# Weight units converted in turn, three weight fetches in front of v's loads, and column sums by bfloat16 matmuls, in a fused attention and feed-forward kernel

## The chip, the core and the metric

The kernel is one program on one core of one Trainium2 chip. The metric is the device time of an execution in microseconds (us). Before the change the median of 3 runs is 866.14 us (863.68 to 867.47). Everything read from a trace below is from one further execution, which took 866.7 us; its first to last instruction spans 865.0 us, so 1.7 us lie around the span.

## What is computed

Random-feature attention over 8 batches, 8 heads, 576 rows of 64 and 128 features, and behind it a bilinear feed-forward block over the 4608 rows of 512:

```python
def phi(x):
    proj = np.einsum('bhsd,md->bhsm', x, omega)
    sq = np.sum(x * x, axis=-1, keepdims=True) / 2.0
    h = proj - sq
    h = h - np.max(h, axis=-1, keepdims=True)
    return np.exp(h) / np.sqrt(m)
q_p, k_p = (phi(q_s), phi(k_s))            # q, k times 64 ** -0.25
kv = np.einsum('bhsm,bhsd->bhmd', k_p, v)
z = np.sum(k_p, axis=2)
num = np.einsum('bhsm,bhmd->bhsd', q_p, kv)
den = np.einsum('bhsm,bhm->bhs', q_p, z)[..., None] + 1e-06
x = num / den                              # heads side by side: 4608 x 512
a = x @ w1                                 # w1, w2: 512 x 1024
b = x @ w2
h = a * b @ w3                             # 1024 x 1024
out = h @ w_out                            # 1024 x 512
```

The four weight matrices arrive as float64, q, k, v and omega as float32.

## The kernel before

**Tiles.** The 4608 rows are 36 chunks of 128. For each chunk the k side makes features (`features`, `k_chunk`), `kv_batch` sums k features times v over a batch of 4.5 chunks, the q side makes features (`q_chunk`), a transposing DMA on the SP queue turns them (`eqT`), `q_attend` multiplies them with `kv` (the tile `nu`), `x_turn` scales and turns the result (`xT`), `gate` makes x @ w1 and x @ w2 (the tiles `ab`, line 636) and their product, and `project_out` multiplies that with the folded matrix w3 @ w_out (the tiles `o`, line 665). Most products run as three float16 passes over a high and a low part; the first 9 chunks of k and the first 5 of q are multiplied in float32 instead (line 276).

**Weights.** A weight unit is 1 MB of float64. `from_float64` fetches it with a DMA issued by ACT (line 486) into one of three raw buffers of the tile `arena`, takes the absolute value on ACT (line 494, two buffers), and puts a float32 together in four VectorE instructions (lines 500, 502, 503, 504). There are 20 units, and the string `ORDER` says in which order they come: `o` is a quarter of w_out, `W` an eighth of w3, `1` and `2` a quarter of w1 and of w2, `a`, `b` and `S` the splits into float16 parts (`w12_split`, `W_split`). A `W` unit has a float32 product with w_out behind it on TensorE (`product`, the tiles `wp`, lines 574 and 576), whose result ACT copies (line 588). A `1` or `2` unit has its magnitudes summed by a matmul with ones (line 528); the split waits for that sum. A unit's five steps are a tick apart (`SKEW`), and `PER` says how many ticks each slot of the attention's plan takes.

**Norms.** `power_of_two` (line 162) turns sums of squares into a power of two by which q, k, v, omega or the folded matrix are scaled. The sum over the 128 partitions is a matmul of a 128 x 128 float32 matrix of ones with 1, 3 or 8 float32 columns (line 165).

**Order.** `put` files each step in a slot of a plan, the loop at line 812 emits weights, gate units and plan in turn, and the program's scheduler then sets each engine's own order, which the engine keeps. A DMA issued by ACT or SP stands in that engine's queue like any other instruction: one that waits holds up all behind it. The tile `om_raw` of omega's parts lies in `Wb`, and its norm and split stand at the program's head (lines 200 to 206). `v_load` puts v's chunks on the SP queue.

Of the kernel before, what the change touches and what calls it, by code (L numbers as in the profile page):

```python
# [9 lines left out]
F32 = mybir.dt.float32  # L10
F16 = mybir.dt.float16
BF16 = mybir.dt.bfloat16
I32 = mybir.dt.int32
U32 = mybir.dt.uint32
AF = mybir.ActivationFunctionType
ALU = mybir.AluOpType
# [3 lines left out]
P = 128  # L20
# [21 lines left out]
DK = "1111111110"  # L42


ORDER = "ooWWWW11a22booWWWW11a22bS"
SKEW = [0, 1, 2, 3, 4]

PER = [3, 1, 0, 1, 0, 1, 1, 0, 1, 0, 1, 1, 0, 1, 1, 0, 1, 1, 1, 1, 1] + 12 * [1]
# [4 lines left out]
EARLY = 6  # L53
KV_LAG = 5
K_LATE = 8
RAW64_BUFS = 3
O_BUFS = 2
RAW_BUFS = 2
# [10 lines left out]
def tile_favor_attention_then_bilinear_ffn(  # L69
# [19 lines left out]
    nc = tc.nc  # L89
# [12 lines left out]
    SCALE = 1.0 / math.sqrt(math.sqrt(D))  # L102
    TOK = GROUP * P

    const = ctx.enter_context(tc.tile_pool(name="const", bufs=1))
# [9 lines left out]
    def bank_m(name):  # L115
        return ps_m.tile([P, 512], F32, tag="pm", name=name)
# [5 lines left out]
    make_identity(nc, ident)  # L122
    ones_bf = const.tile([P, P], BF16, name="ones_bf")
    nc.vector.memset(ones_bf, 1.0)
    ones = const.tile([P, P], F32, name="ones")
    nc.vector.memset(ones, 1.0)
    ln_e = const.tile([P, 1], F32, name="ln_e")
    nc.vector.memset(ln_e, 15 * math.log(2.0))

# [22 lines left out]
    def square_sum(out, src, name, pre=1.0):  # L152

        n = src.shape[1] * (src.shape[2] if len(src.shape) > 2 else 1)
        junk = at.tile([P, 512], BF16, tag="junk", name=f"junk_{name}", bufs=1)
        r0, rows = 0, src.shape[0]
        dst = junk[r0 : r0 + rows, 0:n]
        if len(src.shape) > 2:
            dst = dst.rearrange("p (i j) -> p i j", i=src.shape[1])
        nc.scalar.activation(dst, src, AF.Square, scale=pre, accum_out=out)  # L160

    def power_of_two(cols, n, name, pre=1.0, add=False, bufs=4):

        bank = bank_m(f"norm_{name}")
        nc.tensor.matmul(bank[:, 0:n], ones, cols, start=True, stop=True)
        t = bank[:, 0:n]
        if add:
            total = small("total")
            nc.vector.tensor_reduce(total, t, AX.X, ALU.add)
            t, n = total, 1  # L170

        q = bank[:, 16 : 16 + n]
        p = bank[:, 32 : 32 + n]

        nc.vector.tensor_scalar(
            q.bitcast(I32), t.bitcast(I32), 24, 23, ALU.logical_shift_right, ALU.logical_shift_left
        )
        nc.vector.tensor_scalar(p, q, 2.0**50 / pre, 2.0**-77 / pre, ALU.mult, ALU.max)
        s = small(f"s{n}_{bufs}", n, bufs=bufs)
        nc.vector.reciprocal(s, p)  # L180
        return p, s
# [13 lines left out]
    om_raw = Wb[:, 0, 0:M]  # L195
    nc.sync.dma_start(om_raw[0:D], omT)
    nc.sync.dma_start(om_raw[D:P], omT)
    om = const.tile([P, 2, M], F16, name="om")
    om_sq = const.tile([P, 1], F32, name="om_sq")
    square_sum(om_sq, om_raw, "om")  # L200
    pom, som = power_of_two(om_sq, 1, "om")
    nc.scalar.mul(om[:, 0], om_raw, som)
    nc.vector.scalar_tensor_tensor(om[:, 1], om_raw, som, om[:, 0], ALU.mult, ALU.subtract)

    unom = const.tile([P, 1], F32, name="unom")
    nc.vector.tensor_scalar_mul(unom, pom, SCALE)

    def chunks_of(b):

# [5 lines left out]
    def load(src, c, name):  # L215
        t = at.tile([P, NP, P], F32, tag=f"{name}raw", name=f"{name}raw_{c}", bufs=RAW_BUFS)
        nc.sync.dma_start(t, src[c])
        raws[name, c] = t
# [39 lines left out]
    def features(c, name):  # L258


        if whole(c, name):
            raw, es = raws.pop((name, c)), SCALE
        else:
            hl, es = hls.pop((name, c))
        pg = banks(f"{name}pj_{c}").rearrange("p g (i m) -> p g i m", m=M)
        pj = pg.rearrange("p g i m -> p (g i) m")

        def project(first=None):
            for i in range(NP):
                if first is not None:  # L270
                    for g in range(2):
                        nc.tensor.matmul(pg[:, g, i], ident, first(g * NP + i), start=True, stop=False)
                if whole(c, name):
                    for g in range(2):
                        d = slice(g * D, (g + 1) * D)
                        nc.tensor.matmul(  # L276
                            pg[:, g, i], raw[d, i], om_raw[d], start=first is None, stop=True
                        )
                    continue
                for n, (x, y) in enumerate(PASSES):  # L280
                    for g in range(2):
                        d = slice(g * D, (g + 1) * D)
                        nc.tensor.matmul(  # L283
                            pg[:, g, i],
                            hl[d, x, i],
                            om[d, y],
                            start=first is None and n == 0,
                            stop=n == len(PASSES) - 1,
                        )

        project()
        if whole(c, name) and c + 2 < NCH:
            load(srcs[name], c + 2, name)
        nm = small("nm", H)
        nc.vector.tensor_reduce(nm, pj, AX.X, ALU.max, negate=True)  # L295
        e = at.tile([P, H, M], F32, tag="e", name=f"{name}e_{c}", bufs=2)
        kind = pick(DK if name == "k" else DQ, c)
        if kind == "2":

            project(lambda h: nm[:, h : h + 1].broadcast_to([P, M]))  # L300
            nc.scalar.activation(e, pj, AF.Exp, scale=es, bias=ln_e)
        elif kind == "1":

            nc.vector.tensor_scalar(nm, nm, es, 15 * math.log(2.0), ALU.mult, ALU.add)
            for h in range(H):
                nc.scalar.activation(e[:, h], pj[:, h], AF.Exp, scale=es, bias=nm[:, h : h + 1])
        else:
            nc.vector.tensor_tensor(e, pj, nm.unsqueeze(2).broadcast_to([P, H, M]), ALU.add)  # L308
            nc.scalar.activation(e, e, AF.Exp, scale=es, bias=ln_e)  # L309
        return e  # L310
# [9 lines left out]
    ek, vhl, vraw, pv, kvs = {}, {}, {}, {}, {}  # L320

    def k_chunk(c):
        e = features(c, "k")
        ek[c] = at.tile([P, 2, H, M], F16, tag="ek", name=f"ek_{c}", bufs=EK_BUFS)
        in_parts(ek[c], e, pick(EH, c), pick(EL, c))

    def v_load(c):
        vraw[c] = at.tile([P, H, D], F32, tag="vraw", name=f"vraw_{c}", bufs=VRAW_BUFS)
        nc.sync.dma_start(vraw[c], v[c])

    vam, sv = {}, {}

# [135 lines left out]
        return free.pop(0)  # L468

    left = {}  # L470

    def used(at):

# [4 lines left out]
    def from_float64(new, src, name):  # L478

        st = {}  # L480

        def fetch():
            at = st["at"] = raw_at.pop(0)
            raw = arena[:, at : at + 4].bitcast(U32).rearrange("p b i -> p (b i)")

            nc.scalar.dma_start(raw.rearrange("p (j i) -> p j i", j=src.shape[1]), src)
            st["raw"] = raw.rearrange("p (i t) -> p i t", t=2)

        def magnitude():

            at = st["mag"] = mag_at.pop(0)
            st["g"] = arena[:, at : at + 2].rearrange("p b i -> p (b i)")
            st["dst"] = new()
            nc.scalar.activation(st["g"], st["raw"][:, :, 1].bitcast(F32), AF.Abs)

        def bits():
            g = st["g"]
            top, low = st["raw"][:, :, 1], st["raw"][:, :, 0]

            nc.vector.tensor_scalar(g, g, F64_TOP, F64_LEAST, ALU.min, ALU.max)  # L500
            g = g.bitcast(U32)
            nc.vector.tensor_scalar(g, g, 3, 0x3FFFFFFF, ALU.logical_shift_left, ALU.bitwise_and)
            nc.vector.scalar_tensor_tensor(g, top, 0xC0000000, g, ALU.bitwise_and, ALU.bitwise_or)  # L503
            nc.vector.scalar_tensor_tensor(  # L504
                st["dst"].bitcast(U32), low, 29, g, ALU.logical_shift_right, ALU.bitwise_or
            )
            raw_at.append(st["at"])
            mag_at.append(st["mag"])

        return [fetch, magnitude, bits]  # L510
# [203 lines left out]
    units, seen = [], {}  # L714
    for ch in ORDER:
        n = seen.get(ch, 0)
        seen[ch] = n + 1
        st = make[ch](n)
        units.append([None] * 3 + st + [None] if len(st) == 1 else st + [None] * (5 - len(st)))
    behind = sorted(range(5), key=lambda k: -SKEW[k])  # L720
    ticks = [
        [units[t - SKEW[k]][k] for k in behind if 0 <= t - SKEW[k] < len(units) and units[t - SKEW[k]][k]]
# [17 lines left out]
    def put(slot, rank, fn):  # L740
        plan.setdefault(slot, []).append((rank, len(plan[slot]) if slot in plan else 0, fn))
# [65 lines left out]
        step(i)  # L807
    for c in range(2):
        load(kT, c, "k")
    put(begin[-1] - 3, 11, lambda: load(qT, 0, "q"))  # L810
    put(begin[-1] - 2, 11, lambda: load(qT, 1, "q"))
    for t in range(max(plan) + 1):
        n = min(PER[t] if t < len(PER) else 1, len(ticks))
# [53 lines left out]
```

## Time and profile before

| what | value |
|---|---|
| median of 3 runs | 866.14 us |
| the profiled execution | 866.7 us, span 865.0 us |
| TensorE (PE) busy | 789.3 us, 91% |
| VectorE (DVE) busy | 594.4 us, 69% |
| ScalarE (ACT) busy | 455.0 us, 53% |
| GpSimd (POOL) busy | 222.0 us, 26% |
| chain that ended last | PE 81%, DVE 8%, DMA 4%, ACT 4%, issue 2% |
| moved by DMA | 88.40 MB, mean 102 GB/s |

The page gives shares of the whole span. Since the first 300 us hold all weight work and the rest holds none, a share says little of either; the rows below are therefore taken by stretch. "Granted clock" is the TensorE clock as a share of its full 2.4 GHz: 1.00 is 2.4, 0.50 is 1.2. A releaser is what an engine's instruction waited for last.

### The profile page before, as it was taken

To read this page: it belongs to the slowest core of one execution; us is meant where nothing else is said; L and a number is where in the kernel's file an instruction comes from. 1 tells how busy PE (TensorE), PEld (TensorE's weight loads), DVE (VectorE), ACT (ScalarE), POOL (GpSimd) and SP (SyncE) were. 2 spreads that over 40 slices of the span, in tenths; PEclk is the share of its full clock that TensorE was granted. 3 is DMA by queue.
4 is the path that set the end of the run, shared out by engine and by line. 5 is a ranking of instruction groups with operands and counts; after the bars stand their busy time and mean duration, and the time that the engine had idled before them with its cause. 6 is when DMAs were issued, how large, how long until landed. Compare 5 with 4: busy or idle time off the path is not lost.

```text
span 865.0 us, 20229 instructions
## 1 busy us (share of the span) xinstructions
PE 789.3 (91%) x8479; PEld 585.1 (68%) x8484; DVE 594.4 (69%) x1066; ACT 455.0 (53%) x813; POOL 222.0 (26%) x220
## 2 busy tenths in 40 slices
PE   2876399489996899999999999999999999999998
PEld 2344255387875777777777777877777777777774
DVE  5778887887879877777877777778777754652200
ACT  2667566758456665655565656555655443322221
POOL 0000010222333433334333334343333342222110
PEclk9996599699998999999999999999999999999999
DMA  8455646432444643644534434335342343332100
GB/s 328 150 191 164 196 129 190 119 59 62 87 112 102 96 115 95 98 75 98 123 86 87 111 98 99 74 89 133 87 87 62 62 80 81 63 62 49 37 14 36
DMA packets 142522, 88.40 MB, mean 102 GB/s; under 512 B 116704, under 2 KB 116832, under 8 KB 142432
## 3 DMA queue, kind: packets, MB, share of 16 engines
q1 hardware_dynamic: 134944, 66.15, 33.7%
q10 hardware_dynamic: 7488, 20.97, 7.3%
q8 instruction: 66, 1.08, 0.5%
q14 instruction: 24, 0.20, 0.1%
HBM read 49.35 MB, written 9.44 MB: 68 GB/s over the span
## 4 chain that ended last, share of the span: by engine, by line
PE 81%; DVE 8%; DMA 4%; ACT 4%; issue 2%; POOL 0%; SPq 0%; ACTq 0%; DVEq 0%
PE ab L636 40%; PE o L665 20%; PE wp L576 7%; PE nu L401 3%; PE kvp L366 3%; PE qpj L283 2%; PE kpj L283 2%; DMA kraw<-kT 1%; DVE nm L295 1%; DMA eqT<-eq 1%; PE wp L574 1%; DMA qraw<-qT 1%; DVE w12b L504 1%; DVE arena L503 1%; PE kpj L276 1%
## 5 line engine op out<-in xcount | busy, mean ns | idle before, releaser
L636 PE MATMUL ab<-xT,w12b 128*128 128x256 f16 (+1 forms) x3840 | 396.0, 263 | 10.4 <-DMA xT<-xhl 7.1
L636 PEld LDWEIGHTS <-w12b 128*128 128x128 f16 x3840 | 342.7, 99 | 51.7 <-issue 9.0
L665 PE MATMUL o<-Wb,arena 128*128 128x512 f16 x864 | 193.6, 379 | 1.1 <-DVE Wb L146 0.6
L651 POOL TENSOR_TENSOR arena<-asb,arena 128x512 f16<-128x512 f32 x72 | 84.5, 1174 | 294.9 <-ACT arena L650 294.4
L665 PEld LDWEIGHTS <-arena 128*128 128x128 f16 x864 | 84.3, 100 | 94.6 <-issue 1.5
L318 POOL TENSOR_TENSOR eq<-qe,eq 128x1024 f16<-128x1024 f32 x34 | 73.9, 2172 | 141.2 <-DVE eq L132 86.8
L646 DVE TENSOR_TENSOR asb<-ab,asb 128x512 f32<-128x512 f32 x72 | 49.4, 687 | 62.9 <-PE ab L636 62.5
L650 ACT CAST arena<-asb 128x512 f16<-128x512 f32 x72 | 44.3, 615 | 85.5 <-DVE asb L646 85.5
L318 POOL TENSOR_TENSOR ek<-ke,ek 128x1024 f16<-128x1024 f32 x28 | 59.7, 2131 | 103.2 <-ACT ek L134 62.2
L576 PE MATMUL wp<-w12b 128*128 128x512 f32 x128 | 60.9, 631 | 13.5 <-DVE w12b L504 13.5
L309 ACT ACTIVATE qe<-qe,ln_e,es 128x1024 f32<-128x1024 f32 x31 | 38.4, 1240 | 47.6 <-DVE qe L308 47.6
L146 DVE SCALAR_TENSOR_TENSOR khl<-kraw,s,khl 128x512 f16<-128x512 f32 x27 | 49.3, 1827 | 16.2 <-ACT khl L143 16.2
L576 PEld LDWEIGHTS wp<-w12b 128*128 128x128 f32 x128 | 25.6, 203 | 45.7 <-issue 31.3
L309 ACT ACTIVATE ke<-ke,ln_e,es 128x1024 f32<-128x1024 f32 x27 | 33.5, 1241 | 42.9 <-DVE ke L308 42.9
L146 DVE SCALAR_TENSOR_TENSOR qhl<-qraw,s,qhl 128x512 f16<-128x512 f32 x31 | 27.9, 899 | 37.7 <-ACT qhl L143 37.7
L401 PEld LDWEIGHTS <-eqT 128*128 128x128 f16 (+1 forms) x960 | 32.4, 101 | 29.0 <-DMA eqT<-eq 19.4
L401 PE MATMUL nu<-kv,eqT 128*128 128x65 f16 (+1 forms) x960 | 34.8, 196 | 18.5 <-DMA eqT<-eq 18.5
L160 ACT ACTIVATE junk_q<-qraw 128x512 bf16<-128x512 f32 x31 | 19.5, 630 | 60.4 <-DMA qraw<-qT 60.4
L645 ACT ACTIVATE asb<-ab 128x512 f32<-128x512 f32 x72 | 42.0, 584 | 16.1 <-PE ab L636 11.0
L437 ACT ACTIVATE xhl<-xs,p2r 128x512 f16<-128x512 f32 x36 | 25.9, 719 | 41.1 <-DVE p2r L189 40.1
L295 DVE TENSOR_REDUCE nm<-kpj 128x8 f32<-128x1024 f32 x36 | 43.8, 1217 | 3.6 <-PE kpj L276 3.3
L132 DVE CAST eq<-qe 128x1024 f16<-128x1024 f32 x31 | 21.5, 693 | 34.2 <-ACT qe L309 34.2
(127 smaller groups left out, 996.2 us busy)
## 6 DMA issues: line engine op xcount, KB each, us to landing
kraw<-kT SPq DMA_DIRECT2D x36, 256.0 KB, 2.7
vraw<-v SPq DMA_DIRECT2D x36, 256.0 KB, 3.5
qraw<-qT SPq DMA_DIRECT2D x36, 256.0 KB, 2.7
out<-o SPq DMA_DIRECT2D x36, 256.0 KB, 2.2
arena<-w3T ACTq DMA_DIRECT2D x8, 1024.0 KB, 5.2
arena<-w ACTq DMA_DIRECT2D x8, 1024.0 KB, 6.0
arena<-wo ACTq DMA_DIRECT2D x4, 1024.0 KB, 6.1
eqT<-eq SPq DMA_TRANSPOSE x72, 3.1
```

Source lines behind the costliest of these rows:

```text
L146: nc.vector.scalar_tensor_tensor(lo, src, s, hi, ALU.mult, ALU.subtract)
L295: nc.vector.tensor_reduce(nm, pj, AX.X, ALU.max, negate=True)
L309: nc.scalar.activation(e, e, AF.Exp, scale=es, bias=ln_e)
L318: (nc.vector if lo == "d" else nc.gpsimd).tensor_tensor(t[:, 1], e, t[:, 0], ALU.subtract)
L401: nc.tensor.matmul(nu[r0:r1, h // 4, h % 4], t[:, x, place(h), r0:r1], kvs[b][:, y, h], start=n == 0, stop=n == 2,)
L576: nc.tensor.matmul(ps, w[:, j, k * P : (k + 1) * P], guest[:, j], start=j == j0, stop=j == HALF - 1,)
L636: nc.tensor.matmul(ps[:, k], w12[m][i][cc][:, a, r * P : (r + 1) * P], x[:, b, cc, off : off + T], start=j == 0, stop=j == len(mm) - 1,)
L645: nc.scalar.mul(asb, ab[0], 2.0**-37)
L646: nc.vector.tensor_tensor(asb, ab[1], asb, ALU.mult)
L650: nc.scalar.copy(h[:, 0], asb)
L651: nc.gpsimd.tensor_tensor(h[:, 1], asb, h[:, 0], ALU.subtract)
L665: nc.tensor.matmul(ps, hs[c, f][0][:, a], W[f][:, b], start=i == 0, stop=i == len(mm) - 1)
```

## The change

Three things change. First, `ORDER` puts a unit of w1 or w2 behind each of the first four units of w3, where these four stood in a row; from the second `oo` on the string is the same. Second, what stands at the front: the first three units' fetches are issued ahead of all else, omega's norm and split are a function that the plan calls in slot 11, v's first load waits for the end of the first conversion, and the VectorE part of the first k chunk's features stands behind the second conversion. Third, the matmul with ones in `power_of_two` takes bfloat16 ones and, of each float32 column entry, the upper 16 bits, read as bfloat16.

```diff
-ORDER = "ooWWWW11a22booWWWW11a22bS"
+ORDER = "ooW1W1aW2W2booWWWW11a22bS"
...
+OM_AT = 11
+K_BEHIND = 1
...
-    ones = const.tile([P, P], F32, name="ones")
-    nc.vector.memset(ones, 1.0)
...
-        nc.tensor.matmul(bank[:, 0:n], ones, cols, start=True, stop=True)
+        nc.tensor.matmul(bank[:, 0:n], ones_bf, cols.bitcast(BF16)[:, 1::2], start=True, stop=True)
...
-    square_sum(om_sq, om_raw, "om")
-    pom, som = power_of_two(om_sq, 1, "om")
-    nc.scalar.mul(om[:, 0], om_raw, som)
-    nc.vector.scalar_tensor_tensor(om[:, 1], om_raw, som, om[:, 0], ALU.mult, ALU.subtract)
-
     unom = const.tile([P, 1], F32, name="unom")
-    nc.vector.tensor_scalar_mul(unom, pom, SCALE)
+
+    def om_split():
+
+        square_sum(om_sq, om_raw, "om")
+        pom, som = power_of_two(om_sq, 1, "om")
+        nc.scalar.mul(om[:, 0], om_raw, som)
+        nc.vector.scalar_tensor_tensor(om[:, 1], om_raw, som, om[:, 0], ALU.mult, ALU.subtract)
+        nc.vector.tensor_scalar_mul(unom, pom, SCALE)
...
     def k_chunk(c):
-        e = features(c, "k")
+        if c == 0:
+            with tc.issue_after(converted[K_BEHIND]):
+                e = features(c, "k")
+        else:
+            e = features(c, "k")
...
-        nc.sync.dma_start(vraw[c], v[c])
+        dma = nc.sync.dma_start(vraw[c], v[c])
+        if c == 0:
+
+            tc.add_manual_dep(
+                dma.ins,
+                converted[0].name,
+                mybir.DependencyInfo(mybir.DependencyClass.Sync, mybir.DependencyReason.DATA),
+                reason="v_load",
+            )
...
+    for u in units[:RAW64_BUFS]:
+        u[0]()
+        u[0] = None
...
+    put(OM_AT, 4, om_split)
```

`converted` is a list of the last instruction of each conversion (line 504 before, 520 after). The changed kernel has its lines moved down: the fetch is line 501, the absolute value 509, the four conversion instructions 515 to 520, the `wp` product 593, the sum of magnitudes 545, the folded product `o` 682; line 165 stays.

ACT's queue at the program's start, before (wo, w3T and w are the DMAs that fetch units of w_out, w3, and w1 or w2; Wb holds omega's parts here):

```order
L486 DMA arena<-wo 128x2x1024
L160 ACT_TABLE_LOAD
L160 ACTIVATE junk_om,om_sq<-Wb 128x128
L486 DMA arena<-wo 128x2x1024
L202 ACTIVATE om<-Wb,s_4_95 128x128
L494 ACTIVATE arena<-arena 128x1024
L486 DMA arena<-w3T 128x4x512
L494 ACTIVATE arena<-arena 128x1024
L306 ACTIVATE ke_152<-kpj_139,nm 128x128 x3
```

and after:

```order
L501 DMA arena<-wo 128x2x1024 x2
L501 DMA arena<-w3T 128x4x512
L509 ACT_TABLE_LOAD
L509 ACTIVATE arena<-arena 128x1024 x3
L501 DMA arena<-w 128x2x1024
L501 DMA arena<-w3T 128x4x512
L509 ACTIVATE arena<-arena 128x1024
L308 ACTIVATE ke_139<-kpj_126,nm 128x128 x8
```

Three fetches and three absolute values stand ahead of the first exponentials (`ke`), and omega's two instructions are gone from here.

TensorE's order from the first product on, before (kpj are projections of k chunks, l sums of magnitudes of w1 or w2 units):

```order
L576 MATMUL wp_0_165<-w12b 128x512 x4
L576 MATMUL wp_1_170<-w12b 128x512 x4
L576 MATMUL wp_0_193<-w12b 128x512 x4
L576 MATMUL wp_1_198<-w12b 128x512 x4
L576 MATMUL wp_0_243<-w12b 128x512 x4
L576 MATMUL wp_1_248<-w12b 128x512 x4
L276 MATMUL kpj_261<-Wb,kraw_148 128x128 x8
L576 MATMUL wp_0_291<-w12b 128x512 x4
L576 MATMUL wp_1_296<-w12b 128x512 x4
L528 LDWEIGHTS ones_bf
L528 MATMUL l_0_0_312<-wab_0_0_310,ones_bf 128x512
```

and after:

```order
L593 MATMUL wp_0_152<-w12b 128x512 x4
L593 MATMUL wp_1_157<-w12b 128x512 x4
L545 LDWEIGHTS ones_bf
L545 MATMUL l_0_0_182<-wab_0_0_180,ones_bf 128x512
L545 LDWEIGHTS ones_bf
L545 MATMUL l_0_0_182<-wab_0_0_180,ones_bf 128x512
L593 MATMUL wp_0_222<-w12b 128x512 x4
L593 MATMUL wp_1_227<-w12b 128x512 x4
L278 MATMUL kpj_239<-Wb,kraw_135 128x128 x8
L278 MATMUL kpj_321<-Wb,kraw_199 128x128 x8
```

The first sum of magnitudes stands behind one product in place of four; the third and fourth product stand behind the projections of three k chunks, omega's and v's norm.

TensorE at one of the later norms, before:

```order
L665 LDWEIGHTS arena
L665 MATMUL o_2921<-Wb,arena 128x512
L165 MATMUL norm_q_k_2949<-sums_101,ones 128x3
L401 LDWEIGHTS eqT_2631
L401 MATMUL nu_2962<-kv_1866,eqT_2631 128x65
```

and after:

```order
L682 LDWEIGHTS arena
L682 MATMUL o_2919<-Wb,arena 128x512
L165 LDWEIGHTS ones_bf
L165 MATMUL norm_q_k_2947<-sums_88,ones_bf 128x3
L415 LDWEIGHTS eqT_2629
L415 MATMUL nu_2960<-kv_1864,eqT_2629 128x65
```

The place is the same; the float32 matmul, which brings its own weights, is a load of weights and a matmul in bfloat16. On VectorE, ACT, SP and TensorE the orders are the same, row by row, from the split of the first q features (`eq`) on, but for these norms and one pair of instructions on ACT that changes places.

## Rows read from the trace of the kernel before

**Rows 1.** Stretches: length, PE, PEld, DVE, ACT, POOL busy, granted clock, DMA share, GB/s.

```profile
60.00:105.00 45.00, 18.66 (x203) 12.98 (x204) 38.17 (x57) 30.19 (x62) 0.64 (x10) 0.66 0.61 195
...
207.00:289.00 82.00, 72.49 (x961) 56.07 (x961) 66.16 (x117) 47.76 (x83) 24.45 (x14) 0.96 0.40 94
289.00:865.00 576.00, 572.16 (x6276) 434.14 (x6276) 365.17 (x681) 277.63 (x457) 177.70 (x160) 1.00 0.37 82
```

**Rows 2.** VectorE from first k maximum to end of eq: its busy time.

```profile
10.40:95.50 85.10, 71.86 (x100) 0.88 0.57 190
```

**Rows 3.** Waits of VectorE in that stretch: us in total, times, longest.

```profile
DVE arena L500 <- ACT arena L494: 3.9, 2, 3.5
DVE w12b L504 <- PE wp L576: 2.7, 2, 2.3
```

**Rows 4.** Timeline, VectorE: start, us, line, operation, [idle before <- releaser].

```profile
10.46 1.23 DVE L295 TENSOR_REDUCE nm<-kpj 128x8 f32<-128x1024 f32 x1 [0.95 <-PE kpj L276]
...
17.16 0.69 DVE L500 TENSOR_SCALAR arena<-arena 128x1024 f32<-128x1024 f32 x1
...
21.01 0.69 DVE L500 TENSOR_SCALAR arena<-arena 128x1024 f32<-128x1024 f32 x1
...
94.31 1.22 DVE L318 TENSOR_TENSOR eq<-qe,eq 128x1024 f16<-128x1024 f32 x1
...
103.94 0.17 DVE L410 TENSOR_SCALAR gd<-nu 128x8 f32<-128x8 f32 x1 [3.56 <-PE nu L401]
```

**Rows 5.** Timeline, ACT's start.

```profile
0.74 0.42 ACTq L486 DMA_DIRECT2D arena<-wo  x1
6.22 1.28 ACT L160 ACT_TABLE_LOAD   x1 [6.22 <-DMA Wb<-omT]
...
9.80 1.11 ACT L494 ACTIVATE arena<-arena 128x1024 f32<-128x1024 f32 x1
```

**Rows 6.** DMAs issued from 0 to 5 us: median us to landing.

```profile
arena<-wo ACTq DMA_DIRECT2D x1, 1024.0 KB, 5.1
```

**Rows 7.** DMA queues (q10 ACT's, q1 SP's), 9 to 12 us: packets, MB, share.

```profile
q10 hardware_dynamic: 190, 0.78, 64.8%
q1 hardware_dynamic: 252, 0.45, 39.8%
```

**Rows 8.** Timeline, TensorE: the products of w3 units with w_out.

```profile
25.00 23.41 PE L576 MATMUL wp<-w12b 128*128 128x512 f32 x48 [12.86 <-DVE w12b L504]
...
105.29 8.79 PE L576 MATMUL wp<-w12b 128*128 128x512 f32 x16 [0.66 <-DVE w12b L504]
...
115.10 7.13 PE L576 MATMUL wp<-w12b 128*128 128x512 f32 x16
```

**Rows 9.** Timeline, TensorE, about one norm.

```profile
330.42 0.90 PE L401 MATMUL nu<-kv,eqT 128*128 128x65 f16 x24
331.15 5.40 PE L636 MATMUL ab<-xT,w12b 128*128 128x256 f16 x48
336.49 0.84 PE L283 MATMUL qpj<-om,qhl 64*128 64x128 f16 x24
337.26 5.41 PE L636 MATMUL ab<-xT,w12b 128*128 128x256 f16 x48
342.61 0.84 PE L283 MATMUL kpj<-om,khl 64*128 64x128 f16 x24
343.38 0.39 PE L165 MATMUL norm_q_k<-sums,ones 128*128 128x3 f32 x2
343.63 0.59 PE L665 MATMUL o<-Wb,arena 128*128 128x512 f16 x2
```

**Rows 10.** Line 165 from 289 us on: min/median/max ns, first to last start.

```profile
L165 PE MATMUL norm_q_k<-sums,ones x40: 252/262/273, 306.4 to 672.0; 128*128 128x3 f32 x40
...
L165 PE MATMUL norm_v<-vam,ones x10: 256/256/256, 312.5 to 659.5; 128*128 128x8 f32 x10
...
L165 PE MATMUL norm_q<-sums,ones x10: 171/252/273, 690.3 to 764.0; 128*128 128x3 f32 x10
```

More of the change, by code (lines that the diff above doesn't have):

```diff
@@ L470, in tile_favor_attention_then_bilinear_ffn @@
     left = {}
+    converted = []
     def used(at):
@@ L503, in bits @@
             nc.vector.scalar_tensor_tensor(g, top, 0xC0000000, g, ALU.bitwise_and, ALU.bitwise_or)
-            nc.vector.scalar_tensor_tensor(
-                st["dst"].bitcast(U32), low, 29, g, ALU.logical_shift_right, ALU.bitwise_or
+            converted.append(
+                nc.vector.scalar_tensor_tensor(
+                    st["dst"].bitcast(U32), low, 29, g, ALU.logical_shift_right, ALU.bitwise_or
+                ).ins
             )
```

## The prediction

> **What bounds the kernel now.** The page's shares say little, so I read the stretches first [rows 1]. From 289 us to the end TensorE is busy 572.2 of 576 us at the full clock, VectorE 365: there every TensorE microsecond is a microsecond of the kernel. From 207 to 289 TensorE stands idle 9.5 of 82 us, so what it saves there is not sure to shorten anything. From 60 to 105 it is busy 18.7 of 45 us at a granted clock of 0.66, while VectorE is busy 38.2: the start is VectorE's, with waits. Second, VectorE's own account over the start, from the first maximum of k's features to the end of the first `eq` split: 85.1 us, of them 71.9 busy and 13.2 idle [rows 2]. Third, what ends its idle time: absolute values of fetched units that ACT makes late (3.9 us), and products that still read the block a conversion wants to write (2.7) [rows 3]; the rest is small pieces. That `eq` split matters since all behind it waits: eqT is transposed, nu follows, VectorE sits 3.56 us until nu comes [rows 4], and only behind that the fifth product starts, at 105.29 [rows 8].
>
> **The change, part by part: the front.** Before, ACT's queue stops at omega's transfer until 6.22 us, loads its table (1.28 us), sums omega's squares, and makes its first absolute value at 9.80 [rows 5], though the first unit, issued at 0.74, landed 5.1 us later, at 5.8 [rows 6]. VectorE's conversions come behind the maximum at 10.46 [rows 4]. After, ACT waits for the unit alone: 5.84 + 1.28 + 1.11 = 8.2 us, where VectorE starts converting. A conversion costs 21.01 - 17.16 = 3.85 us [rows 4]. No instruction is saved on VectorE up to `eq`, but a memset: its 71.9 us stay, they start at 8.2 instead of 10.4.
>
> The second and third fetch share the DMA engines with the first loads of k, and with q's, which SP's order now has ahead of v's. In a stretch where both queues had work, ACT's moved 0.78 MB in 3 us and SP's 0.45 [rows 7]; at 0.26 MB/us the second megabyte, begun when the first has landed at 5.8, lands near 9.6, its absolute value is there at 10.7, and VectorE, through with its first two instructions at 9.6, waits 1.0 us. The Trainium skill ("DMA: Bandwidth & Descriptors", section "Queues, rings and completion order") has the DMA engines take packets of the queues in turn; by it the share would be about what those rows show, and had it not held, the wait would lie between 0 and 2.3 us. The first product can then start at 8.2 + 3 x 3.85 + 2 x 1.23 (maxima) + 1.0 = 23.2 us, before at 25.00 [rows 8].
>
> v's loads, which stand behind the first conversion now, are first read by sums of squares that ACT has behind the exponentials of the second k chunk; omega's parts are first read by the tenth chunk of k. So both moves cost nothing, hidden by the conversions and products between; with that cover gone a late v would hold ACT up by one landing, 5.1 us [rows 6].
>
> **The order of the units.** A `W` unit costs VectorE 3.85 us and TensorE 7.13 (warm, the last product of [rows 8]), a `1` or `2` unit VectorE 3.85 and TensorE one short sum. Four `W` in a row made VectorE wait for TensorE; in turn, a pair costs 7.7 us on VectorE and some 8 on TensorE. So the 2.7 us of waits on products go. What is late next: I walked along the new order of VectorE and ACT with the durations of the trace, and find the waits 1.0 (second fetch), 0.6 (the sixth unit, whose fetch stands on ACT behind a cast of `ek`), 0.7 (`ek`), 3.4 (the third k chunk's projection now stands behind both first products, so its maximum comes late), 0.6 (third `W` unit) and 2.3 in small pieces: 8.6 us. Such a walk sees only the waits one thinks of. The lower end is therefore 8.6, the upper the 13.2 of before, and I take 11.0, the middle. `eq` then ends at 8.2 + 71.9 + 11.0 = 91.1 instead of 95.5: a lead of 4.4 us, with ends 2.0 (8.2 + 71.9 + 13.2 = 93.3, less rounding) and 6.8 (88.7). From there on all orders are as before, so the lead passes from wait to wait (eqT, nu, the fifth product, and so on) to 289 us, where TensorE takes over. The collision of eqT with the sixth and seventh `W` fetch is in both kernels.
>
> **The norms.** From qpj to the next products is 337.26 - 336.49 = 0.77 us; from kpj to the norm 0.77 as well, and from the norm to the product behind it 343.63 - 343.38 = 0.25 [rows 9]. So a float32 norm takes 0.25 us of TensorE's stream. Behind 289 us there are 30 (two records each, 60 together [rows 10]): 20 of q and k, 5 of v, and 5 of q alone, the shortest of which is a third shorter, for which I take 0.1: 25 x 0.25 + 5 x 0.1 = 6.8 us in all. No row shows a bfloat16 matmul of 3 columns. The nearest is nu: 24 matmuls of 65 columns, each with a weight load, in 331.15 - 330.42 = 0.73 us, 0.03 each [rows 9]. The other end is 0.25, nothing gained. I take 0.05, near the closer row: 30 x 0.05 = 1.5, saved 5.3 us, ends 0 and 6.8. Norms before 289 us I put at nothing, since TensorE has slack there. VectorE, which takes the sums, is busy 365 of 576 us behind 289 [rows 1] and loses nothing.
>
> **Sum.** 866.7 (the profiled execution, span 865.0) - 4.4 - 5.3 = 857.0. That execution lies 0.6 above the median, so against the median it is 856.4; I say 856.5.
>
> **Rivals.** *The lead is lost, the norms count.* ACT's order puts some fetches directly ahead of the absolute values of the same or the next unit, and each fetch takes 5.1 us to land [rows 6]; if three such waits fall on VectorE, as 3.9 us of such waits do before [rows 3], the 2.2 us of earlier start and the 2.7 of freed waits are gone. Against it: ACT has slack, 30.2 busy of 45 us [rows 1]. Time 866.1 - 5.3 = 860.8.
>
> *The norms count nothing*, the case in which the change does not do what it says: the load of bfloat16 ones and a matmul whose columns lie two apart could hold the stream as long as the float32 pair. Against it speaks the 0.03 us of nu. Time 866.1 - 4.4 = 861.7. With both gains gone it is 866.
>
> *Slower: the products lose the clock.* In one row, 48 records take 23.41 us; a product that starts behind a long idle time takes 8.79 us, the next, warm, 7.13 [rows 8]. No row shows a product wholly at 1.2 GHz; twice the warm 7.13, 14.3 us, is its upper end. In the new order the third and fourth product stand behind small projections and norms, in a stretch in which TensorE had a granted clock of 0.66 before [rows 1]. If both ran wholly at 1.2 GHz, in place of the 8.8 and 7.1 of my walk, it would cost 5.5 + 7.2 = 12.7 us; and the 18.7 us of matmuls of that stretch would take 18.7 x 0.66 / 0.5 = 24.7, of which I put 2 on the path: 856.5 + 12.7 + 2 = 871.2. It decides from the point where TensorE is at 0.50 through both and q's projection comes more than 10 us late. Against it: a product behind idle time was back at speed after a fraction of its length [rows 8]. The Trainium skill ("TensorE: Matmul & The Clock Gate", section "HAM oscillation — how this bites in real kernels") warns of gaps between matmuls since the clock falls in them; the trace agrees (busy 18.7 of 45 us, clock 0.66 [rows 1]), and by that rule alone the change, which takes four products apart, would be this rival.
>
> **How the numbers follow.** Both gains 0.52 (856.5, own range 853 to 861); lead lost 0.20 (860.8); norms nothing 0.12 (861.7); neither 0.07 (866); slower 0.09 (871.2). What a measurement of this kernel can tell from no change is about 0.5%, 4.3 us. Faster, below 861.8: nearly all of the first, most of the second, half of the third: 0.73; slower, above 870.5: 0.08; the same 0.19. A range of 8 in 10 leaves out the slower case, a tenth at most, and the best ends of both gains: 850.5 (866.1 less 6.8 and 6.8, with 2 for an unforeseen gain) to 865.5.
>
> **What would show it.** First conversion at 8.2 us (wrong if behind 10); first product near 23; `eq` ended near 91 (wrong if behind 95); the idle time of VectorE from the first conversion to there near 11 us; the granted clock between 45 and 80 us not at 0.50 through two whole products; from kpj to the product behind a norm 0.8 us instead of 1.02; the stretch that began at 289 us shorter by 5 us. I am wrong if that last stretch keeps its 576 us, or if `eq` comes no earlier.

## The result and the profile after

The changed kernel takes 857.13 us (median of 4 runs, 855.41 to 857.38), the kernel before 866.09 beside it: a ratio of 0.9891, 95% interval [0.9867, 0.9915]. 856.5 was forecast, in a range of 850.5 to 865.5. Its profiled execution took 857.33 us, span 855.4; before these were 866.7 and 865.0.

Stretches of the changed kernel, with the columns of [rows 1]:

```profile
25.00:60.00 35.00, 21.84 (x89) 10.55 (x88) 27.99 (x46) 24.95 (x56) 0.00 (x0) 0.80 0.45 147
60.00:105.00 45.00, 30.64 (x237) 17.93 (x236) 38.19 (x57) 28.71 (x57) 0.67 (x10) 0.81 0.64 203
285.10:855.40 570.30, 566.53 (x6246) 428.47 (x6246) 365.31 (x681) 277.97 (x457) 177.76 (x160) 1.00 0.36 83
```

and of the kernel before, from 25 to 60 us, in which three of the four products stood close together:

```profile
25.00:60.00 35.00, 34.83 (x117) 16.57 (x118) 25.45 (x33) 22.42 (x45) 0.00 (x0) 1.00 0.44 140
```

The last stretch begins with the same work, the sums of a later block of keys (`kvp`), 3.87 us earlier than before (288.97), and takes 570.3 us instead of 576.0 [rows 1]: 5.7 saved. The two add to the 9.6 us of the span.

VectorE's account, from the first conversion to the end of the first `eq` split, for comparison with [rows 2]:

```profile
8.81:92.08 83.27, 51.02 (x314) 27.90 (x314) 72.05 (x104) 52.69 (x112) 0.67 (x10) 0.89 0.59 198
```

Busy 72.05 of 83.27, so 11.2 us idle, where it was 13.2. Read as an account, the end of `eq` comes 3.4 us earlier (92.08 for 95.50): 1.6 of earlier start (8.81 for 10.40) and 2.0 of less idle time, less 0.2 of added work. Such an account does not say what the kernel would lose without the early start; the experiments do. The waits behind the idle time, to set beside [rows 3] (us in total, times, longest); of the first row's 11.3 us, 6.45 lie before the first conversion:

```profile
DVE arena L515 <- ACT arena L509: 11.3, 9, 6.5
DVE nm L297 <- PE kpj L278: 3.0, 1, 3.0
DVE nm L297 <- PE qpj L278: 1.5, 1, 1.5
```

The waits for a product to release its block (2.7 us in [rows 3]) are gone. A wait of 3.0 for the third k chunk's projection and one of 1.5 for q's stand in their place, and what VectorE waits for ACT's absolute values behind the first one, 11.3 - 6.45 = 4.9, is more than the 3.9 of before. VectorE's timeline at the places of [rows 4]:

```profile
8.81 0.69 DVE L515 TENSOR_SCALAR arena<-arena 128x1024 f32<-128x1024 f32 x1 [6.45 <-ACT arena L509]
...
10.56 0.69 DVE L515 TENSOR_SCALAR arena<-arena 128x1024 f32<-128x1024 f32 x1 [0.33 <-ACT arena L509]
...
41.70 1.23 DVE L297 TENSOR_REDUCE nm<-kpj 128x8 f32<-128x1024 f32 x1 [2.99 <-PE kpj L278]
...
90.85 1.23 DVE L320 TENSOR_TENSOR eq<-qe,eq 128x1024 f16<-128x1024 f32 x1
...
100.05 0.17 DVE L424 TENSOR_SCALAR gd<-nu 128x8 f32<-128x8 f32 x1 [2.42 <-PE nu L415]
```

The start of ACT, where [rows 5] were:

```profile
0.74 0.97 ACTq L501 DMA_DIRECT2D arena<-wo  x2
5.96 0.37 ACTq L501 DMA_DIRECT2D arena<-w3T  x1
6.36 1.28 ACT L509 ACT_TABLE_LOAD   x1 [6.36 <-DMA arena<-wo]
7.66 1.12 ACT L509 ACTIVATE arena<-arena 128x1024 f32<-128x1024 f32 x1
9.38 1.15 ACT L509 ACTIVATE arena<-arena 128x1024 f32<-128x1024 f32 x1 [0.60 <-DMA arena<-wo]
```

The third fetch is issued only at 5.96 us, and the table load stands behind it. TensorE's products, where [rows 8] were; the third had its unit converted at 52.4 but stands behind omega's norm:

```profile
22.43 8.82 PE L593 MATMUL wp<-w12b 128*128 128x512 f32 x16 [9.08 <-DVE w12b L520]
33.42 7.13 PE L593 MATMUL wp<-w12b 128*128 128x512 f32 x16 [1.74 <-DVE w12b L520]
...
55.80 0.16 PE L165 MATMUL norm_om<-om_sq,ones_bf 128*128 128x1 bf16 x1 [9.05 <-ACT junk_om L160]
...
55.85 9.17 PE L593 MATMUL wp<-w12b 128*128 128x512 f32 x16
67.44 7.03 PE L593 MATMUL wp<-w12b 128*128 128x512 f32 x16
...
101.52 8.53 PE L593 MATMUL wp<-w12b 128*128 128x512 f32 x16
```

And TensorE from the start of the last stretch to the first norm in it, where [rows 9] were:

```profile
285.10 5.34 PE L380 MATMUL kvp<-vhl,ek 128*128 128x65 f16 x120 [3.08 <-DVE ke L310]
...
301.74 0.84 PE L285 MATMUL kpj<-om,khl 64*128 64x128 f16 x24
302.51 0.18 PE L165 MATMUL norm_q_k<-sums,ones_bf 128*128 128x3 bf16 x1
302.55 1.67 PE L682 MATMUL o<-Wb,arena 128*128 128x512 f16 x7
```

From the norm's start to the next product is 0.04 us; before it was 0.25.

### The profile page after: what moved, and what is told of

Read it like the earlier page. It is cut to its first block, busy times and chain, and to the rows that moved or that the text cites. A ratio compares the mean times of both kernels' runs of the same rounds, so it can differ in the third digit from the quotient of the medians.

```text
span 855.4 us, 20140 instructions
## 1 busy us (share of the span) xinstructions
PE 780.5 (91%) x8442; PEld 576.5 (67%) x8442; DVE 593.9 (69%) x1065; ACT 454.5 (53%) x813; POOL 222.1 (26%) x220
## 4 chain that ended last, share of the span: by engine, by line
PE 77%; DVE 8%; ACT 6%; DMA 5%; issue 3%; POOL 0%; SPq 0%; ACTq 0%; DVEq 0%
PE ab L653 40%; PE o L682 20%; PE wp L593 5%; PE nu L415 3%; PE kvp L380 3%; PE qpj L285 3%; PE kpj L285 2%; DVE nm L297 1%; DMA kraw<-kT 1%; DMA arena<-w3T 1%; DMA arena<-wo 1%; ACT arena L509 1%; DVE w12b L520 1%; DVE arena L518 1%; PE qpj L278 1%
## 5 line engine op out<-in xcount | busy, mean ns | idle before, releaser
L653 PE MATMUL ab<-xT,w12b 128*128 128x256 f16 (+1 forms) x3840 | 396.0, 263 | 10.4 <-DMA xT<-xhl 7.0
L682 PEld LDWEIGHTS <-arena 128*128 128x128 f16 x864 | 82.1, 98 | 94.2 <-issue 0.9
L415 PE MATMUL nu<-kv,eqT 128*128 128x65 f16 (+1 forms) x960 | 34.8, 196 | 15.0 <-DMA eqT<-eq 11.8
L297 DVE TENSOR_REDUCE nm<-qpj 128x8 f32<-128x1024 f32 x36 | 43.8, 1218 | 2.5 <-PE qpj L278 1.7
```

Of the source, the lines that this page charges most:

```text
L415: nc.tensor.matmul(nu[r0:r1, h // 4, h % 4], t[:, x, place(h), r0:r1], kvs[b][:, y, h], start=n == 0, stop=n == 2,)
L653: nc.tensor.matmul(ps[:, k], w12[m][i][cc][:, a, r * P : (r + 1) * P], x[:, b, cc, off : off + T], start=j == 0, stop=j == len(mm) - 1,)
L682: nc.tensor.matmul(ps, hs[c, f][0][:, a], W[f][:, b], start=i == 0, stop=i == len(mm) - 1)
```

## The experiments

The theory taken from these rows: the norms pay behind 289 us and nowhere else; the 3.9 us of lead come from the start and the order together. The rival: one of the two makes the lead alone. `kvp` below is the product that begins the last stretch. Times are medians, brackets are 95% intervals, and the places of `eq` and `kvp` are where they start in one execution.

### The norms alone: e1 and e5

```diff
 # e1: the kernel before, with all norms in bfloat16
-        nc.tensor.matmul(bank[:, 0:n], ones, cols, start=True, stop=True)
+        nc.tensor.matmul(bank[:, 0:n], ones_bf, cols.bitcast(BF16)[:, 1::2], start=True, stop=True)
...
 # e5: the same, but only for the first 12 norms of the program
+        if len(norms_done) <= EARLY_NORMS:
...
```

> The kernel before, with nothing changed but the matmul with ones in power_of_two, which takes bfloat16 ones and the upper halves of the column entries. Theory (the norms and the front are two gains that add up, and a norm counts only where TensorE is the bound): the stretch from the sixth-batch kvp at 289 us to the end is 576.0 us before and 570.3 after the whole change, so it is 570.3 here; the start is as before (eq split at 94.3, that kvp at 289.0). Time 866.1 - 5.7 = 860.4. Rival 1, norms are on the path everywhere: 42 norms of 0.20 us each, 866.1 - 8.4 = 857.7, and the kvp at 286.5. Rival 2, the late stretch got shorter for another reason (the new start changes its states): 866.1.

> The kernel before with the bfloat16 matmul of ones for the first 12 norms in the program's order and the float32 one for the other 30: the cheap norms only where TensorE has slack. Theory (norms ahead of 289 us are worth nothing): the kvp that begins TensorE's stretch stays at 288.6 to 289.0 and the stretch keeps 576.0; the time is that of the kernel before. Rival (a norm is worth its 0.20 us wherever it stands): 12 x 0.20 = 2.4 us less, a ratio of 0.997, kvp at 286.6.

Measured: e1 860.31 us beside 867.82, ratio 0.9919 [0.9900, 0.9938]; e5 864.27 beside 865.29, 0.9989 [0.9973, 1.0005]. The last stretch of each, from `kvp` to the end, e1:

```profile
288.55:858.80 570.25, 566.54 (x6246) 428.49 (x6246) 365.85 (x681) 277.94 (x457) 177.26 (x160) 1.00 0.36 83
```

and e5:

```profile
287.69:863.70 576.01, 572.20 (x6276) 434.20 (x6276) 365.75 (x681) 278.04 (x457) 177.28 (x160) 1.00 0.36 82
```

The stretch is 5.75 us shorter in e1, with 30 TensorE records fewer, and unchanged in e5. Its start hardly moves (288.55 and 287.69, before 288.97). So the norms behind 289 us are worth 5.7 us, and in the time the early ones cannot be told from nothing. In the traces one early norm does show. Omega's norm stands at the head of these kernels, and the first conversion, in the kernel before at

```profile
13.31 0.68 DVE L500 TENSOR_SCALAR arena<-arena 128x1024 f32<-128x1024 f32 x1
```

starts at 12.64 in e1 and 12.87 in e5; `eq` comes at 93.84 and 93.51, before at 94.31. (e3 below, with the float32 norm, has its first conversion at 13.32, and e9, with bfloat16, at 12.83.) These are small shifts: two executions that do the same work can differ by as much, as e8 shows.

### The start and the order taken apart: e2, e3 and e4

```diff
 # e2: the changed kernel with float32 norms (start and order)
-        nc.tensor.matmul(bank[:, 0:n], ones_bf, cols.bitcast(BF16)[:, 1::2], start=True, stop=True)
+        nc.tensor.matmul(bank[:, 0:n], ones, cols, start=True, stop=True)
...
 # e3: the kernel before with the new order alone
-ORDER = "ooWWWW11a22booWWWW11a22bS"
+ORDER = "ooW1W1aW2W2booWWWW11a22bS"
 # e4: e2 with the old order (the start alone)
-ORDER = "ooW1W1aW2W2booWWWW11a22bS"
+ORDER = "ooWWWW11a22booWWWW11a22bS"
```

> The changed kernel with the float32 matmul of ones put back in power_of_two: the new order of the units and the new front alone. Theory: eq split at 90.9 as in the changed kernel, the kvp that begins TensorE's stretch at 285.1 to 285.4, the stretch 576.0 again; time 866.1 - 3.8 = 862.3. Rival 1, part of the earlier start comes from the cheaper norms of omega and v: eq split at 92 or later, time 864. Rival 2, start and norms are not independent (an earlier start is given back in the 207 to 289 us stretch unless the norms are short): the kvp back at 289, time 866.

> The kernel before with the new ORDER string alone; fetches, omega's split, v's loads and the norms stay. Theory of the prediction's sum (half of the lead is the earlier first conversion, half are waits of VectorE that go): first conversion at 13.3 us as before, first product at 25, VectorE's idle time from the first maximum to the eq split 11 us in place of 13.2, eq split near 92.1; time 866.1 - 2.2 = 863.9. Rival 1, the order is all of the lead: eq split at 90.9, 862.3. Rival 2, the order moves waits only, the front is all: eq split at 94.3, 866.1.

> The changed kernel with the old ORDER string and the float32 norms: three fetches first, omega's split in slot 11, v's loads and the first maxima behind conversions. Theory: first conversion at 8.8 us, first product near 22.4, the four products of w3 units then run one behind another as before with VectorE waiting for them (2.7 us), eq split near 92.1; time 866.1 - 2.2 = 863.9. Rival 1, the front is all of the lead: 862.3. Rival 2, the front alone gains nothing, as VectorE only waits longer for the products: eq split at 94.3, 866.1.

Measured, all beside 867.82 us: e2 862.36, ratio 0.9934 [0.9913, 0.9956]; e3 862.64, 0.9945 [0.9923, 0.9966]; e4 866.58, 0.9986 [0.9970, 1.0003]. The `eq` split of e2, e3 and e4 came at 91.72, 92.07 and 93.33, `kvp` at 285.61, 285.95 and 287.52. (e4's profiled execution, 863.84 us, was well below its median; its `kvp` ran at the full clock, which is told at the end.)

By its ratio the order alone is worth 4.8 us (2.9 to 6.7), more than the 2.2 that the prediction's sum leaves for it. The start alone is worth 1.2 us (2.6 to -0.3), and behind the order 0.3 by the medians, with an uncertainty of more than 2 us: neither can be told from nothing, but these times do not rule out the 2.2 us of the sum either. So e3 came out as its first rival, in which the order is all of the lead; e4 lies between its theory and its second rival; and e2, by `eq`, between its theory and its first rival. In the traces the order alone brings `kvp` forward by 3.0 us, the start alone by 1.4, and both together by 3.4; each of these is one execution, and `kvp` is a rough mark (e8). The start does come early: in e4 the first conversion is at 8.91 and the first product at 22.43, 2.6 us before [rows 8]; VectorE's idle time up to `eq` then grows from 13.2 to 14.0 us. The waits on products, 2.7 us before, are 0.4 in e4 though the order is the old one, so they go with the start too, and other waits grow in their place.

How the order alone makes its lead was not as I thought. In e3 VectorE waits (the two largest that are new, from 8 to 95 us):

```profile
DVE l1m L539 <- PE l L528: 5.5, 1, 5.5
DVE nm L295 <- PE kpj L276: 4.6, 2, 3.6
```

and behind `eq`:

```profile
92.07 1.22 DVE L318 TENSOR_TENSOR eq<-qe,eq 128x1024 f16<-128x1024 f32 x1
...
98.67 0.16 DVE L410 TENSOR_SCALAR gd<-nu 128x8 f32<-128x8 f32 x1
```

VectorE from its first maximum to the end of `eq`, with the columns of [rows 2] and those ahead of them:

```profile
10.47:93.29 82.82, 53.48 (x296) 28.14 (x294) 69.99 (x98) 51.47 (x106) 0.67 (x10) 0.91 0.57 192
```

Its idle time is 12.8 us, before 13.2: the 2.7 us of freed waits were taken by new ones. What shrank is the work in front of `eq`, 70.0 us instead of 71.9: two splits of w1 and w2 (0.74 each) now stand behind it, where VectorE had waited 3.56 us for nu [rows 4] and now waits for nu no longer. In the changed kernel this is not so: the work in front of `eq` is 72.05 us, VectorE still waits 2.42 us for nu, and its lead is one of less waiting. Where the start is early the order's lead is therefore read from an account and not isolated.

### Parts of the start taken away: e6 and e7

```diff
 # e6: the changed kernel, v's first load waits for nothing
-            tc.add_manual_dep(
...
 # e7: the changed kernel, the first k chunk's features wait for nothing
-            with tc.issue_after(converted[K_BEHIND]):
...
```

> The changed kernel without the wait of v's first load for the first conversion: v's five chunks (1.25 MB) go out on SP's queue right behind the first two of k. Theory (the engines' bandwidth is shared by the queues, so v slows the second and third fetch): the third unit's absolute value ends at 17 to 18 us in place of 15.3, the first product starts near 24 in place of 22.4, some of it is absorbed, the eq split comes 0 to 1.5 us later; time 0 to 1.5 us above the changed kernel's 857.1. Rival 1, the wait does nothing, as the weights go ahead of v anyhow: same times. Rival 2, it carries most of the front: eq split back at 93 or later, 860.

> The changed kernel without the rule that puts VectorE's part of the first k chunk behind the second conversion: both maxima come first on VectorE. They need the projections, which ended at 13.4 us in the changed kernel. Theory (VectorE's start counts): the first conversion starts behind 13 us in place of 8.8; of the 4.3 us that it stands idle 2.4 are made up by the maxima done in front and some 1 by fetches that VectorE would have waited for; first product near 24, eq split up to 1.5 us later; time 857.1 + 0 to 1.5. Rival, the later waits hide all of it: eq split at 90.9 and 857.1; rival 2, the full 4.3 us come through: 861.4.

Measured beside 865.29 us: e6 854.33, ratio 0.9874 [0.9849, 0.9899]; e7 854.78, 0.9874 [0.9845, 0.9903]. TensorE's first two products in e7:

```profile
28.03 9.11 PE L589 MATMUL wp<-w12b 128*128 128x512 f32 x16 [10.41 <-DVE w12b L516]
37.97 7.13 PE L589 MATMUL wp<-w12b 128*128 128x512 f32 x16 [0.62 <-DVE w12b L516]
```

The first product is 5.6 us later than in the changed kernel, and in e6 3.3 (25.69). In e6 the shared bandwidth of the theory is not the reason: from 4 to 9 us the two queues moved as much as in the changed kernel (ACT's 1.53 and 1.51 MB, SP's 0.48 in both). It is that ACT's third fetch was issued only at

```profile
9.54 0.37 ACTq L493 DMA_DIRECT2D arena<-w3T  x1
```

instead of 5.96, so that the table load came at 9.95 and the first conversion at 12.41. Yet `eq` came at 90.73 in e7 and 91.21 in e6, `kvp` at 284.01 and 284.53. A first product up to 5.6 us later cost nothing that these runs show; that is strong evidence that the early start bought next to nothing.

### The table load made earlier: e8

```diff
...
+    nc.scalar.activation(warm, ln_e, AF.Abs)
```

> The changed kernel with one more activation of a 128 x 1 tile behind ACT's first three fetches, so that ACT loads its table while the first unit is still on its way; in the changed kernel the table load started at 6.36, when the first unit had landed, and took 1.28 us. Theory (VectorE's start counts until the next fetch binds): first conversion near 7.5 in place of 8.8; the second unit, whose absolute value ends at 10.5, then binds, so the first product comes 0 to 0.4 us earlier and the time stays within 0.5 us of 857.1. Rival 1, the 1.3 us come through to the end: eq split at 89.6, 855.8. Rival 2, the third fetch, held back on ACT until 5.96, comes later for it and the start gets longer.

Measured: 854.95 us beside 865.29, 0.9883 [0.9855, 0.9912]. But the load of the table did not move:

```profile
6.01 0.37 ACTq L502 DMA_DIRECT2D arena<-w3T  x1
6.42 1.28 ACT L741 ACT_TABLE_LOAD   x1 [6.42 <-DMA arena<-wo]
7.71 0.20 ACT L741 ACTIVATE warm<-ln_e 128x1 f32<-128x1 f32 x1
```

ACT was still held by the third fetch, issued at 6.01 us. The experiment tells nothing on the table load. It tells how far two executions lie apart, since e8 is the changed kernel but for an activation of 0.20 us: `eq` came at 91.53, 0.7 us later than in the changed kernel, and `kvp` 3.4 us earlier:

```profile
281.71 3.81 PE L381 MATMUL kvp<-vhl,ek 128*128 128x65 f16 x120 [3.06 <-DVE ke L311]
```

So a difference of up to 3 us between single places of `kvp` proves nothing; the times and their intervals decide.

### The order and the norms without the start: e9

```diff
 # the kernel before, with two of the three changes
-ORDER = "ooWWWW11a22booWWWW11a22bS"
+ORDER = "ooW1W1aW2W2booWWWW11a22bS"
-        nc.tensor.matmul(bank[:, 0:n], ones, cols, start=True, stop=True)
+        nc.tensor.matmul(bank[:, 0:n], ones_bf, cols.bitcast(BF16)[:, 1::2], start=True, stop=True)
```

> The kernel before with the new order of the units and the bfloat16 norms, without anything of the new front. Theory A (the earlier start is absorbed by later waits, and the two other gains add): the eq split near 92 us, kvp near 286, the stretch behind it 570, span near 855.7 (865.0 less 3.1 of the order alone less 6.2 of the norms alone), ratio 0.987 to 0.991, as the changed kernel. Theory B (the earlier start carries half of the lead): the eq split near 93.1, kvp near 287.2, span 857.5 or more, ratio 0.992.

Measured: 855.85 us beside 867.82, ratio 0.9863 [0.9836, 0.9889], span 855.3. `eq` at 91.83, `kvp` at 283.87. Theory A: without anything of the new start the kernel is as fast as the changed one (0.9891 [0.9867, 0.9915]). Had the start been worth 2.2 us, e9's ratio would lie 0.0025 above the changed kernel's; it lies 0.0028 below, and the two intervals together allow for some 0.0036. By the span the sum is close too: 865.0 - 3.1 (e3) - 6.2 (e1) = 855.7, though single executions scatter by more than that agreement: `kvp` came 2.1 us earlier than in e3, with `eq` only 0.2 earlier, and took 6.46 us instead of 5.35.

### Two waits removed: e10, e11 and e12

```diff
 # e10: the third k chunk's projection ahead of the second product
-PER = [3, 1, 0, 1, 0, 1, 1, 0, 1, 0, 1, 1, ...
+PER = [3, 1, 0, 1, 0, 1, 1, 0, 0, 0, 2, 1, ...
 # e11: omega's norm and split later in the plan
-OM_AT = 11
+OM_AT = 20
 # e12: both
```

> The changed kernel with the projection of the third k chunk ahead of the second W product on TensorE, so that VectorE's maximum of it does not wait 2.99 us as it does at 41.70. Theory A (what VectorE saves at the start is taken back by later waits): that wait goes, the eq split comes at 90 to 91.5 us and the time is within 0.3% of the changed kernel's. Theory B (VectorE's waits add up to the end of eq): the eq split near 88, kvp near 282.5, some 3 us faster than the changed kernel, ratio to the kernel before 0.986.

> The changed kernel with omega's split emitted nine places later in the plan, so that its norm no longer stands ahead of the third product, which waits for it until 55.8 us though its unit is converted at 52.4. Theory A: the third product starts at 52.4 to 53, 3 us earlier, but the eq split keeps 90.9 within 0.6 us and the time stays within 0.3% of the changed kernel's. Theory B (products are what VectorE's later conversions wait for): the eq split 2 to 3 us earlier, near 88, the time 2 to 3 us less.

> The changed kernel with both edits, the third k chunk's projection ahead of the second product and omega's split nine places later. Theory A (absorbed): the eq split within 1 us of 90.9, the time within 0.3% of the changed kernel's, ratio 0.987 to 0.991. Theory B (each removed wait counts): the eq split near 86, span near 850.5, ratio 0.983.

Measured beside 867.82 us: e10 854.50, ratio 0.9847 [0.9821, 0.9874]; e11 868.37, 1.0019 [0.9999, 1.0039]; e12 867.44, 0.9999 [0.9976, 1.0021].

By its waits and by `eq` e10 went as theory A:

```profile
36.23 1.22 DVE L297 TENSOR_REDUCE nm<-kpj 128x8 f32<-128x1024 f32 x1
...
42.08 1.23 DVE L297 TENSOR_REDUCE nm<-kpj 128x8 f32<-128x1024 f32 x1 [2.29 <-PE kpj L278]
```

```profile
DVE nm L297 <- PE qpj L278: 3.4, 1, 3.4
```

The maximum of the third k chunk (36.23) waits for nothing now, where it had waited 2.99. In its place the fourth chunk's waits 2.29, q's wait grew by 1.9, and `eq` came at 91.12. By its time e10 is 0.4% below the changed kernel's ratio, where A said within 0.3%, and at the 0.986 of theory B or below. Its interval overlaps the changed kernel's, so it is not shown to be faster; B's `eq` at 88 did not come.

e11 and e12 missed both theories: their time is that of the kernel before. The norms' gain is still in it, since the last stretch takes 568.8 us in e11 and 570.2 in e12 (span 864.1 and 866.1); what stands in front of it has become 6 to 7 us longer than before the change. Their third product did come at 52.52 and 49.47. In e11 `eq` came at 93.05, and in e12 it came earlier than in any other kernel here, at 89.94. TensorE behind it, in e12:

```profile
91.90 0.29 PE L415 MATMUL nu<-kv,eqT 128*128 128x65 f16 x2 [9.48 <-ACT junk_v L160]
92.12 1.65 PE L278 MATMUL qpj<-Wb,qraw 64*128 64x128 f32 x12
100.97 1.39 PE L415 MATMUL nu<-kv,eqT 128*128 128x65 f16 x22 [7.20 <-DMA eqT<-eq]
...
107.15 0.19 PE L165 MATMUL norm_om<-om_sq,ones_bf 128*128 128x1 bf16 x1
107.19 2.06 PE L591 MATMUL wp<-Wb,ident 128*128 128x512 f32 x2
109.04 5.02 PE L593 MATMUL wp<-w12b 128*128 128x512 f32 x8
```

and in the changed kernel:

```profile
76.00 1.13 PE L591 MATMUL wp<-Wb,ident 128*128 128x512 f32 x2
...
80.63 2.82 PE L591 MATMUL wp<-Wb,ident 128*128 128x512 f32 x6
84.24 1.16 PE L278 MATMUL kpj<-Wb,kraw 64*128 64x128 f32 x16 [0.79 <-DVE kv L390]
94.28 0.29 PE L415 MATMUL nu<-kv,eqT 128*128 128x65 f16 x2 [8.88 <-DMA eqT<-eq]
...
98.62 1.39 PE L415 MATMUL nu<-kv,eqT 128*128 128x65 f16 x22 [2.90 <-DMA eqT<-eq]
```

There the matmuls that begin the next products (line 591, 3.95 us) fill a hole of TensorE at 76 to 83 us. In e12 they stand behind omega's late norm at 107, the rest of eqT lands 2.4 us later (100.97 for 98.62) though `eq` was earlier, and the first matmul of the fifth product starts at 109.0 for 101.5. The first of the gate's products behind it (line 653) starts at 127.61 for 118.04: by there 9.6 us are lost. `kvp` comes at 295.86, in e11 at 295.34, 10 to 11 us late. So an early `eq` passes its lead on only if what stands behind it on the other engines stays in place. That TensorE's order is what costs these 10 us is read from the two traces; no run puts the line 591 matmuls back with omega's norm left late, and why the planner's other choices moved as they did was not tried.

## Why the prediction was right, and where not

**The sum.** A lead of 4.4 and norms of 5.3 were forecast; 3.87 and 5.73 were measured. In the two traces the lead was carried to 289 us as forecast: 3.9 us at `gd`, the first work behind nu (103.94 and 100.05), 3.8 at the fifth product (105.29 and 101.52), 3.9 at `kvp`. The norms were added to it there, as the theory said (e1, e2, e5 and e9).

**The norms: right, and by its steps.** I took a bfloat16 norm at 0.05 us of TensorE's stream beside 0.25; it was 0.04. The saving of 0.21 per norm times 25, and some 0.1 times 5, gives 5.75, as e1 shows. Norms before 289 us were put at nothing; e5's time agrees (1.0 us less, with an interval that holds none), though omega's norm does bring the old start's first conversion forward by some 0.5 us.

**The account of VectorE: its sum right, its attribution wrong.** The account was 8.2 + 71.9 + 11.0 = 91.1 to the end of `eq`; measured are 8.81 + 72.05 + 11.22 = 92.08. The start was 0.6 late, 0.5 of it since the table load began at 6.36 instead of 5.84, behind the third fetch (below). The second fetch fell as forecast: absolute value from 9.38, VectorE waiting 0.33 instead of 1.0 us. First product at 22.43 (23.2 forecast). The wait on the third k chunk's projection, 3.4 in the forecast, was 2.99. The waits for absolute values, 1.0 and 0.6 in the walk, came to 4.9, and q's projection (1.5) was not in it. The walk itself was 2.6 short; the 11.0, the middle between it and the old waits, was a guess that came out near.

The step that failed is the one that took the 71.9 us and the waits as fixed while the start moves: "its 71.9 us stay, they start at 8.2 instead of 10.4", which credits half of the lead, 2.2 us, to the earlier start. Taken back, that start costs nothing that shows: a first product 5.6 us later leaves `eq` and the time where they were (e7), and without anything of the new start the time is no longer (e9, whose ratio and interval, set against the changed kernel's, rule out the 2.2 us). Added, it gives 0.3 us (e2 against e3) or 1.2 (e4 against before), which cannot be told from nothing. The other term, 2.7 us of waits on products that go, is not what the order gave either: the order alone is worth 4.8 us of time, left VectorE's idle time at 12.8 us (e3), and got its lead at `eq` from work that moved behind it into the wait for nu; and in e4 those waits went without the order, and VectorE's idle time did not shrink. That the two mis-sized terms made the right sum is luck: VectorE's waits are not a fixed amount to which a start is added, since TensorE and the transfers end them at times of their own.

**v's and omega's moves at no cost: no cost of v's shows; omega's is open.** e6, in which v waits for nothing, takes no longer and no less that could be told apart. Omega's norm held a third product that was ready for 3.4 us; what that costs is not shown, since e11, with the norm nine places later, also changes what TensorE does behind `eq` and loses as much as the whole gain.

**The rivals.** The lead lost and the norms without effect did not happen. Slower by the clock: TensorE's granted clock did fall in the stretch from 25 to 60 us, to 0.80 from 1.00, where TensorE is now busy 21.8 us instead of 34.8; but it rose from 0.66 to 0.81 in the next one, where two of the products now are (30.6 us busy, before 18.7). The third product took 9.17 us and the fourth 7.03, none near 14.3. All four took 32.2 us, before 30.5 (23.41 and 7.13), so standing apart cost them 1.6 us on TensorE. The landing of 5.1 us that the first rival gives each fetch was the first fetch's; the one issued from 9 to 12 us, in the stretch of [rows 7], took 9.4.

## What to carry to other kernels

An idle time of the bounding engine belongs to whoever ends it: before a gain from an earlier start is counted, name for each later wait whether its end moves too. Small float32 matmuls with ones on a full TensorE cost their whole length in the stream, 0.25 us here, and in bfloat16 0.04; count them only where TensorE is the bound. And an earlier milestone is a gain only if the work behind it, and the work that filled other engines' holes, stays where it was (e12: `eq` 0.9 us earlier than in the changed kernel, the last stretch 10 us later).

## What the runs showed of the hardware

- **A third 1 MB fetch held ACT.** With two on its queue, issued from 0.74 us, the third was issued at 5.96, about when the first had landed (5.2 us after its issue); ACT did not load its table before 6.36 (6.42 in e8). An activation that was put in front to load the table had no effect for this reason. In e6, with v's five loads on SP's queue as well, the first landed after 5.4 us, at 6.1, and the third was still issued only at 9.54, about when the second had landed (9.4). What releases it was not found.
- **`kvp` at two speeds.** The same 120 matmuls took 5.34 us in the changed kernel (285.10) and 3.80 in e4 (287.52), where the granted clock was 1.00 instead of 0.89. The idle time in front does not decide it: 5.36 us behind 2.66 idle in e5, 3.81 behind 2.65 in e11. The window from 285 to 300 us, the changed kernel's and then e4's:

```profile
285.00:300.00 15.00, 14.90 (x225) 13.71 (x226) 12.66 (x25) 8.96 (x16) 7.52 (x14) 0.89 0.64 108
```

```profile
285.00:300.00 15.00, 12.48 (x217) 11.37 (x218) 13.27 (x26) 10.35 (x18) 7.04 (x14) 1.00 0.60 101
```

What decides it was not found; it is 1.5 us in a span.
